# An attention and gated-MLP kernel on one core: another opening order, value tiles all in paired halves, and a last tile in column halves

## The chip, the core and the metric

The kernel runs on one NeuronCore of a Trainium2 chip. The core has TensorE (matrix products, here with its weight loads shown apart), VectorE, ScalarE, GpSimd and SyncE, which issues the DMA transfers; 16 DMA engines move the data. The metric is the device time of one execution in microseconds (us). Beside the timed runs there is one profiled execution, and all views of the profile come from that one.

## The reference, cut to what matters

```python
def reference(A_x, A_wqkv, A_wo, B_x, B_w_gate, B_w_up, B_w_down, gate_w):
    x = A_x                                                 # 2048 x 512
    g = _sigmoid((x * gate_w).sum(-1, keepdims=True))
    a = _A_ref(x, A_wqkv, A_wo)       # attention, 32 heads of 16: softmax(q k / 4) v, then wo
    b = _B_ref(x, B_w_gate, B_w_up, B_w_down)   # (sigmoid(x w_gate) * (x w_up)) w_down, 1792 wide
    return g * a + (1 - g) * b
```

All inputs are fp32.

## The kernel before, in words

Every fp32 operand of a large product is split into a high part in fp32r and a low part, the rest (`split`, line 108). A product of two such operands is the sum of three: high x high, high x low, low x high (`terms`, line 143). A product with 128 contraction rows uses the whole height of the array; one with 64 rows uses half of it, and two such products on different halves can run side by side. `Sum` (line 152) makes a sum of such halves: `half(0)` uses the lower 64 rows, `half(1)` the upper. Two sums are run as a pair, one on its lower rows while the other is on its upper rows; then they change sides. Both halves of a sum write one PSUM bank, so at the change `turn` (line 172) has the next products wait for a token, an empty GpSimd instruction that itself waits for the last product of the first side.

The stages, in order:

1. **Opening (lines 78 to 94, 243 to 257).** TensorE runs products of zeros while the first data arrive (26 in three forms). SyncE loads the first 128 columns of the Q weights, two contraction tiles of the first 512 tokens, the first 128 columns of the K weights, and the other tiles. ScalarE makes the high parts, VectorE the low ones. GpSimd sets the Q and K buffers (`QS`, `KS`: two of each, 128 x 2048) to their start values.
2. **First projections (lines 582 to 602).** For four chunks of 512 tokens, 12 products each for the first Q and K columns (96 in all). `put_first` splits each result and writes it to DRAM (`q_d`, `k_d`); after every second chunk `load_pair` (line 235) reads those tokens back into `QS` and `KS`, head by head, in 12 transfers.
3. **Value tiles with the first maxima (lines 635 to 661).** The value projection makes 16 tiles of 128 tokens, 24 half products each (or 12 whole ones). In between stand the first row maxima: `first_max` (line 575) takes the next step of a list of 40; a step makes two 48-row score products (one for each of two heads, on different halves of the array) into two of the four `sm` banks, and VectorE reduces each to a maximum. The maxima of the first half of the queries are packed by VectorE and GpSimd (`put_max`, line 290) and sent through DRAM into a row of `QS`. Four score products of the first loop step are made ahead in the last pair (`ahead`).
4. **The loop (from line 827).** 256 steps of score products, exponentials on ScalarE, products with the values, later maxima and the remaining projections. A step is 5.6 us.
5. **The end (from line 943).** The down projection in chunks of 512 tokens, `down` holding one bank for each of four token tiles, over 14 tiles of the hidden width; `finish` mixes the result with the attention part and stores it.

TensorE, ScalarE, VectorE and GpSimd run their instructions in the order of the program (line 50); SyncE's transfers are put in order by the planner of the framework.

The loop of stage 3, before:

```python
    for t in range(2):
        o = bankv()
        product(o, tokens(t))
        put_v(t, o, act)
    for t in range(2, NS, 2):
        two = [Sum(bankv(), tokens(t + a)) for a in range(2)]
        for g in (LOW, UP):
            first_max()
            for m in range(3 * KT):
                two[0].half(g)
                two[1].half(1 - g)
                if m in (5, 11):
                    first_max()
```

Of the kernel before, what the change touches and what calls it, by code (L numbers as in the profile page):

```python
# [12 lines left out]
F32 = mybir.dt.float32  # L13
F32R = mybir.dt.float32r
AF = mybir.ActivationFunctionType
ALU = mybir.AluOpType
# [8 lines left out]
S, D, H, DH, F = 2048, 512, 32, 16, 1792  # L25
P = 128
# [11 lines left out]
NPER = NSTEP // 2  # L38
FREE = NPER - LEAD // 2
EARLY = 3  # L40
HF = NF // 2
LOW, UP = 0, 1

# [2 lines left out]
def gated_mix(ctx, tc, x, xT, wqk, wv, wo, w_gate, w_up, w_down, gate_w, out):  # L46
# [32 lines left out]
    dve.memset(warm, 0.0)  # L79
    z = warm.bitcast(F32R)  # L80

    def zeros(o, a, b, r=slice(0, P)):
        rows, m, n = r.stop - r.start, o.shape[0], o.shape[1]
        pe.matmul(o, a[r].to_broadcast([rows, m]), b[r].to_broadcast([rows, n]), start=True, stop=True)
    low, up = slice(0, 64), slice(64, P)
    for _ in range(2):
        for c in range(4):
            zeros(banks[2][32 * c:32 * c + VW, :256], warm, warm, low)
        for _ in range(2):
            zeros(banks[1][:, :256], z, z, up)  # L90
    for _ in range(4):
        zeros(banks[1][:, :256], z, z)
    for _ in range(2):
        zeros(banks[2], z, z)
    mpads = [keep.tile([P, 32], F32, name=f"mpad{i}") for i in range(2)]
    mpad = turns(mpads)
    den = keep.tile([P, 512], F32, name="den")
# [7 lines left out]
    def mid(name, dt=F32):  # L105
        return keep.tile([P, 4, 512], dt, name=name, tag="mid", bufs=3)

    def split(h, l, src, hi, lo):
        if hi is act:
            act.activation(h, src, AF.Copy)  # L110
        else:
            hi.tensor_copy(h, src)
        lo.tensor_tensor(l, src, h.bitcast(F32), ALU.subtract)  # L113

    def raw_weights(src, shape, name):
        raw = keep.tile(shape, F32, name=name + "r", tag="wr", bufs=2)
# [26 lines left out]
    def terms(ab):  # L143
        for (ah, al), (bh, bl) in ab:
            yield from ((ah, bh), (ah, bl), (al, bh))
# [55 lines left out]
    def load_x(c, raw=None, ks=range(KT)):  # L201
        raw = raw or mid(f"x{c}")
        for k in ks:
            sp.dma_start(raw[:, k, :], xT[c, k])
        return raw

    def split_x(c, raw, ks=range(KT)):
        cols = slice(c * 512, (c + 1) * 512)
        for k in ks:
            split(xh[:, k, cols], xl[:, k, cols], raw[:, k, :], act, dve)  # L210

    def unit(w, c):
        cols = slice(c * 512, (c + 1) * 512)
        return [((w[0][:, k, :], w[1][:, k, :]), (xh[:, k, cols], xl[:, k, cols])) for k in range(KT)]

    FORM = {0: (0, 1, 0), 1: (0, 0, 1)}

    def put_first(o, dst, c):

        if c % 2:  # L220
            e = [keep.tile([P, 512], F32R, name=f"qe{i}_{c}", tag="er", bufs=6) for i in range(2)]
        else:
            e = keep.tile([P, 2, 512], F32R, name=f"qe_{c}", tag="ev", bufs=2)
            e = [e[:, i, :] for i in range(2)]
        act.activation(e[0], o, AF.Copy)
        dve.tensor_tensor(e[1], o, e[0].bitcast(F32), ALU.subtract)
        for i in range(2):
            sp.dma_start(dst[i, :P, c * 512:(c + 1) * 512], e[i].bitcast(F32))
# [14 lines left out]
    act.activation(g1[:, :1], warm, AF.Exp)  # L243
    ones = v.rearrange("p t (h c) -> p t h c", c=VW)[:, :, :, DH]
    pool.memset(ones, 1.0)
    raw_q = raw_cols(wqk, 0, "q0")
    xr = {0: load_x(0, ks=(0, 1))}
    raw_k = raw_cols(wqk, KT, "k0")
    load_x(0, xr[0], (2, 3))
    w_q = split_weights(raw_q, act, dve)  # L250
    for b in range(2):
        pool.memset(KS[b].bitcast(F32), -1.0)
        pool.memset(QS[b].bitcast(F32), 0.0)
    split_x(0, xr[0], (0, 1))
    w_k = split_weights(raw_k, act, dve)
    split_x(0, xr.pop(0), (2, 3))
    xr.update((c, load_x(c)) for c in range(1, NC))

    stat = {}
    mrow = {}  # L260
# [320 lines left out]

    for c in range(NC):
        if c + 1 < NC:
            split_x(c + 1, xr.pop(c + 1))
# [7 lines left out]
        two = [(bank(), list(terms(unit(w, c))), dst) for w, dst in ((w_q, q_d), (w_k, k_d))]  # L592
        for part in ((0, 6), (6, 12)) if c == 0 else ((0, 12),):
            for o, ops, dst in two:
                for m in range(*part):
                    pe.matmul(o, *ops[m], start=(m == 0), stop=(m == len(ops) - 1))  # L596
                if part[1] == 12:
                    put_first(o, dst, c)
# [312 lines left out]
    bankh = turns([maxb[0], banks[0], banks[1]])  # L911
    acc, had = {}, {}

    def finish(t, o, gate):

        c = t // 4
        if c not in acc:
            acc[c] = lp.tile([P, 4, D], F32, name=f"acc{c}", tag="acc")
        a = acc[c][:, t % 4, :]
        if (t, 0) in acc:  # L920
            dve.scalar_tensor_tensor(a, o, gate[:, t:t + 1], a, op0=ALU.mult, op1=ALU.add)
# [21 lines left out]
    for n, (c, f) in enumerate(chunks):  # L943
        if f == 0:
            down = [bankt() for _ in range(4)]
        if n in at:
            heads_out(at[n], heads.pop(at[n]))
        hl = ready[n]
        for t in range(4):
            ops = list(terms([((hl[0][:, a, t * P:(t + 1) * P], hl[1][:, a, t * P:(t + 1) * P]), wd[f + a])  # L950
                              for a in range(2)]))
            for m, (a, b) in enumerate(ops):
                pe.matmul(down[t], a, b, start=(f == 0 and m == 0), stop=(f == NF - 2 and m == 5))  # L953
            if (n, t) == (0, 1):
                values(NPER - 1)
                flush(later)
            if f == NF - 2:
                finish(4 * c + t, down[t], g0)
# [49 lines left out]
```

## Time and profile before

| what | value |
|---|---|
| median of 3 runs | 1696.73 us (1695.27 to 1698.48) |
| the profiled execution's own time | 1696.12 us |
| its span | 1694.3 us |
| TensorE, VectorE, ScalarE, GpSimd busy | 1688.6, 1446.0, 1358.7, 881.0 us |
| DMA over the span | 223.51 MB, mean 132 GB/s |

How to read the views: the chain of waits follows the work that ended last back through time, and each of its rows has a start, a length and what ran. A timeline row has start, length, engine, line of the kernel, operation, tile written `<-` tiles read, and how many instructions are taken together; in brackets stands the idle time ahead of it and what ended that. `PE` is a TensorE product, `PEld` its weight load; the ends of products are modelled, so the distance between two starts is what a product costs. A stretch's row has for each engine the busy time and the number of instructions, then the granted TensorE clock, the DMA share and GB/s. Tiles `st`, `dn` and `sm` are PSUM banks, `stat` the maxima, `p` the exponentials, `v` the values.

### The profile page before, as it was taken

What the parts mean: (1) busy time and instruction counts of PE and PEld (TensorE: products, weight loads), DVE (VectorE), ACT (ScalarE), POOL (GpSimd) and SP (SyncE); (2) the same over time, 40 slices, a digit from 0 to 9 for tenths busy, and PEclk for the clock granted to TensorE, in tenths of its full rate; (3) what the DMA queues carried; (4) which work ended last, traced back from release to release, by engine and by line L of the source; (5) the groups of instructions that cost most, each with busy time, mean ns of one, the idle gap of its engine ahead of it and who ended that gap; (6) DMA issues with size and microseconds to landing.
All of it is one profiled execution on the core that took longest, in us unless ns stands there. A gap on an engine that the chain in (4) does not pass through costs nothing.

```text
span 1694.3 us, 34493 instructions
## 1 busy us (share of the span) xinstructions
PE 1688.6 (100%) x12502; PEld 1034.9 (61%) x12502; DVE 1446.0 (85%) x2332; ACT 1358.7 (80%) x2644; POOL 881.0 (52%) x862
## 2 busy tenths in 40 slices
PE   9999999999999999999999999999999999999999
PEld 7755555555555555555555555555555555568887
DVE  6988888888889999999888888889988888888643
ACT  4188888888989888888889889898988989984321
POOL 1034343447665455555566676676666666643110
PEclk9999999999999999999999999999999999999999
DMA  9311424243755342433635353535343434468852
GB/s 256 88 39 58 95 64 96 64 126 134 200 173 145 117 120 89 115 113 103 191 104 139 108 144 102 145 102 130 112 127 108 132 120 128 145 233 280 265 195 72
DMA packets 126666, 223.51 MB, mean 132 GB/s; under 512 B 23264, under 2 KB 33248, under 8 KB 123616
## 3 DMA queue, kind: packets, MB, share of 16 engines
q1 hardware_dynamic: 126496, 221.31, 45.0%
q8 instruction: 98, 1.61, 0.4%
q14 instruction: 72, 0.59, 0.1%
HBM read 131.33 MB, written 89.92 MB: 131 GB/s over the span
## 4 chain that ended last, share of the span: by engine, by line
PE 98%; POOL 1%; DVE 0%; issue 0%; DMA 0%; SPq 0%; POOLq 0%; DVEq 0%
PE dn L163 30%; PE sm L768 27%; PE sm L279 12%; PE st L630 7%; PE sm L953 5%; PE sm L630 5%; PE st L279 2%; PE dn L953 2%; PE st L953 2%; PE st L150 1%; PE st L163 1%; PE st L596 1%; PE sm L150 1%; DVE stat L281 0%; PE st L768 0%
## 5 line engine op out<-in xcount | busy, mean ns | idle before, releaser
L281 DVE TENSOR_REDUCE stat<-sm 128x1 f32<-128x512 f32 x1310 | 848.2, 683 | 152.4 <-PE sm L630 133.2
L632 ACT ACTIVATE p<-st 128x512 f32<-128x512 f32 x1020 | 617.9, 653 | 1.4 <-PE st L630 1.4
L632 ACT ACTIVATE p<-sm 128x512 f32<-128x512 f32 x1026 | 608.8, 630 | 0.6 <-PE sm L630 0.2
L279 PE MATMUL sm<-ks,qs 48*128 48x512 f32 x1310 | 521.7, 437 | 0.2
L281 DVE TENSOR_REDUCE stat<-st 128x1 f32<-128x512 f32 x738 | 482.2, 681 | 0.1
L768 PE MATMUL sm<-p,v 128*17 128x512 f32 x4032 | 482.1, 595 | 0.0
L630 PE MATMUL sm<-qs,ks 64*128 64x512 f32 x1026 | 427.4, 420 | 0.1
L630 PE MATMUL st<-qs,ks 64*128 64x512 f32 x1020 | 426.5, 419 | 0.2 <-DVE stat L281 0.2
L279 PEld LDWEIGHTS sm<-ks,qs 48*128 48x128 f32 x1310 | 238.1, 184 | 293.8 <-DVE stat L281 211.3
L785 POOL TENSOR_TENSOR sum<-sum,part 128x512 f32<-128x512 f32 x224 | 288.9, 1290 | 180.7 <-PE sm L630 173.0
L279 PE MATMUL st<-ks,qs 48*128 48x512 f32 x738 | 291.4, 395 | 0.0
L773 ACT ACTIVATE part<-sm 128x512 f32<-128x512 f32 x215 | 128.7, 599 | 132.4 <-issue 107.4
L768 PEld LDWEIGHTS sm<-p,v 128*17 128x17 f32 x4032 | 93.5, 96 | 227.2 <-issue 157.4
L630 PEld LDWEIGHTS st<-qs,ks 64*128 64x128 f32 x1020 | 187.7, 184 | 30.0 <-issue 3.4
L630 PEld LDWEIGHTS sm<-qs,ks 64*128 64x128 f32 x1026 | 189.1, 185 | 9.8 <-issue 4.3
L507 POOL TENSOR_TENSOR chain<-chain,chain 128x512 f32<-128x512 f32 x84 | 108.5, 1292 | 114.4 <-PE sm L630 108.7
L507 POOL TENSOR_TENSOR had<-chain,had 128x512 f32<-128x512 f32 x84 | 108.1, 1287 | 58.8 <-PE sm L630 46.1
L279 PEld LDWEIGHTS st<-ks,qs 48*128 48x128 f32 x738 | 137.7, 187 | 0.9 <-ACT v L613 0.3
L507 POOL TENSOR_TENSOR side<-side,side 128x512 f32<-128x512 f32 x28 | 36.2, 1291 | 93.3 <-PE sm L630 76.4
L569 ACT ACTIVATE chain<-dn 128x512 f32<-128x512 f32 x112 | 77.9, 696 | 0.0
L113 POOL TENSOR_TENSOR ol<-ot,oh 128x1024 fp32r<-128x1024 f32 (+1 forms) x8 | 16.4, 2054 | 102.5 <-ACT oh L110 82.2
L140 POOL CAST qe<-qk 128x512 fp32r<-128x512 f32 x24 | 14.6, 610 | 77.4 <-ACT qk L569 77.4
(879 smaller groups left out, 3215.0 us busy)
## 6 DMA issues: line engine op xcount, KB each, us to landing
gul<-gu_d SPq DMA_DIRECT2D x56, 512.0 KB
had<-gu_d SPq DMA_DIRECT2D x84, 256.0 KB
gu_d<-had SPq DMA_DIRECT2D x84, 256.0 KB
gu_d<-side SPq DMA_DIRECT2D x56, 256.0 KB
qs<-q_d SPq DMA_DIRECT2D x90, 128.0 KB
ks<-k_d SPq DMA_DIRECT2D x90, 128.0 KB
pv_d<-sum SPq DMA_DIRECT2D x32, 256.0 KB
gu_d<-far SPq DMA_DIRECT2D x28, 256.0 KB
```

Source lines behind the costliest of these rows:

```text
L150: pe.matmul(o, a, b, start=(i == 0), stop=(i == len(ops) - 1))
L163: mm = pe.matmul(self.o, a[rows], b[rows], start=(self.n == 0), stop=(self.n == 2 * len(self.ops) - 1))
L279: pe.matmul(t, qs[r:r + KM, qt * P:(qt + 1) * P], ks[r:r + KM, g * 512:(g + 1) * 512], start=True, stop=True)
L281: dve.tensor_reduce(stat[half][:, b, qt % 8, g:g + 1], t, axis=AX.X, op=ALU.max)
L507: pool.tensor_tensor(to, u, w, ALU.add)
L569: leave = lambda e, o: act.activation(e, o, AF.Copy)
L630: pe.matmul(o, ks[r:r + KR, (kt + a) * P:(kt + a + 1) * P], qs[r:r + KR, q0:q0 + 512], start=True, stop=True)
L632: act.activation(pt[:, 2 * a + c, :], o, AF.Exp, scale=DH ** -0.5)
L768: pe.matmul(o[32 * c:32 * c + VW, :], v[:, 2 * k % 16 + a, h * VW:(h + 1) * VW], pts[c // 2][:, 2 * a + c % 2, :], start=(a == 0), stop=(a ...
L773: act.activation(e, o, AF.Copy)
L785: pool.tensor_tensor(s, s, e, ALU.add)
L953: pe.matmul(down[t], a, b, start=(f == 0 and m == 0), stop=(f == NF - 2 and m == 5))
```

## The change

It edits three places.

- The opening: nine zero products of one form (128 rows, 512 columns) in place of 26. The first weights come in two transfers, each with two of the four contraction tiles of both the Q and the K columns, in place of one transfer for Q and one for K. The first token tile's high part is made by VectorE. The products of the first chunk go contraction tile by contraction tile, Q and K in turn. The four memsets of `QS` and `KS` wait for the last split of the second token chunk.
- The value tiles: all 16 run as eight pairs; the first two, which ran as whole products, are paired as well. A maximum step stands ahead of the half products 0, 5, 10, 15 and 20 of each pair's 24, five steps a pair in place of six. `put_max` follows as soon as its maxima are asked for.
- The end: the last token tile's down projection is made as two halves of 256 columns in two banks, and each half is finished and stored by itself.

```diff
-    def zeros(o, a, b, r=slice(0, P)):
...
-    for _ in range(2):
-        for c in range(4):
-            zeros(banks[2][32 * c:32 * c + VW, :256], warm, warm, low)
-        for _ in range(2):
-            zeros(banks[1][:, :256], z, z, up)
-    for _ in range(4):
-        zeros(banks[1][:, :256], z, z)
-    for _ in range(2):
-        zeros(banks[2], z, z)
+    for _ in range(WARM):
+        pe.matmul(banks[2], z.to_broadcast([P, P]), z.to_broadcast([P, 512]), start=True, stop=True)
...
-    raw_q = raw_cols(wqk, 0, "q0")
-    xr = {0: load_x(0, ks=(0, 1))}
-    raw_k = raw_cols(wqk, KT, "k0")
-    load_x(0, xr[0], (2, 3))
-    w_q = split_weights(raw_q, act, dve)
-    for b in range(2):
-        pool.memset(KS[b].bitcast(F32), -1.0)
-        pool.memset(QS[b].bitcast(F32), 0.0)
-    split_x(0, xr[0], (0, 1))
-    w_k = split_weights(raw_k, act, dve)
-    split_x(0, xr.pop(0), (2, 3))
+    both = wqk.rearrange("(a n) p k f -> n p a k f", a=2)[0]
+    raw, xr, w_qk = [], {}, []
+    for ks in (slice(0, 2), slice(2, 4)):
+        raw.append(raw_weights(both[:, :, ks, :], [P, 2, 2, P], f"qk{ks.start}"))
+        xr[0] = load_x(0, xr.get(0), range(ks.start, ks.stop))
     xr.update((c, load_x(c)) for c in range(1, NC))
+    for i, r in enumerate(raw):
+        w_qk.append(split_weights(r, act, dve))
+        if i == 0:
+            cols = xh[:, 0, :512], xl[:, 0, :512]
+            split(*cols, xr[0][:, 0, :], dve, dve)
+            split_x(0, xr[0], (1,))
+        else:
+            split_x(0, xr[0], (2, 3))
+    w_q, w_k = [[(h[:, i, k, :], l[:, i, k, :]) for h, l in w_qk for k in range(2)] for i in range(2)]
...
         if c == 0:
+            hold = pool.nop()
+            tc.add_manual_dep(hold.ins, last.ins.name, SYNC, reason="memsets behind the first tokens")
+            for b in range(2):
+                pool.memset(KS[b].bitcast(F32), -1.0)
+                pool.memset(QS[b].bitcast(F32), 0.0)
...
+        if c == 0:
+            order = [(i, 3 * k + m) for k in range(KT) for m in (0, 2, 1) for i in range(2)]
+        else:
+            order = [(i, m) for i in range(2) for m in range(3 * KT)]
+        for i, m in order:
+            o, ops, dst = two[i]
+            end = (i, m) == [x for x in order if x[0] == i][-1]
+            pe.matmul(o, *ops[m], start=(m == 0), stop=end)
+            if end:
+                put_first(o, dst, c)
...
-    for t in range(2):
-        o = bankv()
-        product(o, tokens(t))
-        put_v(t, o, act)
-    for t in range(2, NS, 2):
+    for t in range(0, NS, 2):
         two = [Sum(bankv(), tokens(t + a)) for a in range(2)]
         for g in (LOW, UP):
-            first_max()
             for m in range(3 * KT):
+                if (12 * g + m) % 5 == 0:
+                    first_max()
                 two[0].half(g)
                 two[1].half(1 - g)
-                if m in (5, 11):
-                    first_max()
-                if (0, 0) in mrow and g == UP and m == 2:
+                if (0, 0) in mrow:
                     for _, step in put_max((0, 0)):
                         step()
...
-    def finish(t, o, gate):
+    def finish(t, o, gate, s=slice(0, D)):
...
-            dve.scalar_tensor_tensor(a, o, gate[:, t:t + 1], a, op0=ALU.mult, op1=ALU.add)
-            sp.dma_start(out[t * P:(t + 1) * P, :], a)
+            dve.scalar_tensor_tensor(a[:, s], o[:, s], gate[:, t:t + 1], a[:, s], op0=ALU.mult, op1=ALU.add)
+            sp.dma_start(out[t * P:(t + 1) * P, s], a[:, s])
...
             down = [bankt() for _ in range(4)]
+            if c == NC - 1:
+                down.append(maxb[0])
+                bankh = turns([banks[0], banks[1]])
...
-            for m, (a, b) in enumerate(ops):
-                pe.matmul(down[t], a, b, start=(f == 0 and m == 0), stop=(f == NF - 2 and m == 5))
+            both = [(down[t], slice(0, D))]
+            if (c, t) == (NC - 1, 3):
+                both = [(down[3], slice(0, 256)), (down[4], slice(256, D))]
+            for o, s in both:
+                for m, (a, b) in enumerate(ops):
+                    pe.matmul(o[:, s], a, b[:, s], start=(f == 0 and m == 0), stop=(f == NF - 2 and m == 5))
+                if f == NF - 2:
+                    finish(4 * c + t, o, g0, s)
```

More of the change, by code (lines that the diff above doesn't have):

```diff
@@ L40 @@
 EARLY = 3
+WARM = 9
 HF = NF // 2
@@ L80, in gated_mix @@
     z = warm.bitcast(F32R)
-    def zeros(o, a, b, r=slice(0, P)):
-        rows, m, n = r.stop - r.start, o.shape[0], o.shape[1]
-        pe.matmul(o, a[r].to_broadcast([rows, m]), b[r].to_broadcast([rows, n]), start=True, stop=True)
-    low, up = slice(0, 64), slice(64, P)
-    for _ in range(2):
-        for c in range(4):
-            zeros(banks[2][32 * c:32 * c + VW, :256], warm, warm, low)
-        for _ in range(2):
-            zeros(banks[1][:, :256], z, z, up)
-    for _ in range(4):
-        zeros(banks[1][:, :256], z, z)
-    for _ in range(2):
-        zeros(banks[2], z, z)
+    for _ in range(WARM):
+        pe.matmul(banks[2], z.to_broadcast([P, P]), z.to_broadcast([P, 512]), start=True, stop=True)
     mpads = [keep.tile([P, 32], F32, name=f"mpad{i}") for i in range(2)]
@@ L112, in split @@
             hi.tensor_copy(h, src)
-        lo.tensor_tensor(l, src, h.bitcast(F32), ALU.subtract)
+        return lo.tensor_tensor(l, src, h.bitcast(F32), ALU.subtract)
     def raw_weights(src, shape, name):
@@ L209, in split_x, with rows_of @@
         for k in ks:
-            split(xh[:, k, cols], xl[:, k, cols], raw[:, k, :], act, dve)
+            last = split(xh[:, k, cols], xl[:, k, cols], raw[:, k, :], act, dve)
+        return last
+    def rows_of(w, c):
+        cols = slice(c * 512, (c + 1) * 512)
+        return [(w[k], (xh[:, k, cols], xl[:, k, cols])) for k in range(KT)]
     def unit(w, c):
-        cols = slice(c * 512, (c + 1) * 512)
-        return [((w[0][:, k, :], w[1][:, k, :]), (xh[:, k, cols], xl[:, k, cols])) for k in range(KT)]
+        return rows_of([(w[0][:, k, :], w[1][:, k, :]) for k in range(KT)], c)
     FORM = {0: (0, 1, 0), 1: (0, 0, 1)}
@@ L583, in gated_mix @@
         if c + 1 < NC:
-            split_x(c + 1, xr.pop(c + 1))
+            last = split_x(c + 1, xr.pop(c + 1))
         if c == 0:
+            hold = pool.nop()
[3 more added lines that the diff above has]
+                pool.memset(QS[b].bitcast(F32), 0.0)
             wv_r = mid("wv_r")
@@ L591, in gated_mix @@
                 split(wv_h[:, k, :], wv_l[:, k, :], wv_r[:, k, :], act, dve)
[L592 to L598, printed above, removed]
+        two = [(bank(), list(terms(rows_of(w, c))), dst) for w, dst in ((w_q, q_d), (w_k, k_d))]
+        if c == 0:
[8 more added lines that the diff above has]
+                put_first(o, dst, c)
         if c % 2:
@@ L956, in gated_mix @@
                 flush(later)
-            if f == NF - 2:
-                finish(4 * c + t, down[t], g0)
         if n + 4 < len(chunks):
```

## The prediction

> **What bounds the kernel now.** I read the page first, then the chain of waits over the first 130 us, then the timelines of the places that the diff touches.
>
> ```profile
> span 1694.3 us, 34493 instructions
> ...
> PE 98%; POOL 1%; DVE 0%; issue 0%; DMA 0%; SPq 0%; POOLq 0%; DVEq 0%
> ```
>
> TensorE holds 98% of the chain. From about 91 us on nothing in the diff touches the loop until the last tile, so what counts is how far the start of that loop moves, and the last microseconds. The chain of waits shows the opening (start, length, what):
>
> ```profile
> 0.92 5.48 PE st L84 x26
> 6.40 22.75 PE st L596 x96
> 29.15 2.72 PE dn L150 x12
> ...
> 34.59 0.43 PE sm L279 x2
> ...
> 51.43 1.38 PE st L163 x12
> ...
> 77.38 2.33 DMA max_d<-mhl
> 79.72 0.80 SPq L303
> 80.58 1.94 DMA qs<-max_d
> 82.66 0.47 PE dn L630
> ...
> 91.43 1.84 PE sm L768 x16
> ```
>
> In order: zero products, 96 projections, two plain value tiles (24 products, 34.59 - 29.15 = 5.44 us), then pairs of half-row value products with maxima among them. Twelve half products are six slots: 1.38 / 6 = 0.23 us a slot, and a pair of maxima's products, on the two halves of the rows, takes one slot too. In that stage VectorE sets the pace:
>
> ```profile
> 65.68 9.21 DVE L281 TENSOR_REDUCE stat<-sm 128x1 f32<-128x512 f32 x15
> ```
>
> One reduction each 0.61 us (9.21 / 15), 12 for a pair of value tiles: 7.3 us, against 24 + 6 slots of TensorE, 6.9 us.
>
> The transfers decide when maxima may begin. SyncE's timeline and its waits:
>
> ```profile
> 16.21 1.33 SPq L228 DMA_DIRECT2D q_d<-qe  x2
> ...
> 25.45 3.60 SPq L241 DMA_DIRECT2D qs<-q_d  x6
> 29.09 2.76 SPq L241 DMA_DIRECT2D ks<-k_d  x6
> ...
> SPq L241 <- DMA q_d<-qe: 10.3, 4, 5.2
> ```
>
> The first 1024 tokens of Q are written at 16.2 to 17.5 us but the read back starts at 25.45, after a wait for those writes. The stretches say why (the last two numbers are the DMA share and GB/s):
>
> ```profile
> 15.00:20.00 5.00, 5.00 (x24) 4.14 (x23) 3.26 (x6) 2.84 (x7) 0.00 (x0) 1.00 1.02 344
> 20.00:25.00 5.00, 5.00 (x24) 4.14 (x23) 4.91 (x9) 4.14 (x8) 0.00 (x0) 1.00 1.08 261
> 25.00:30.00 5.00, 5.00 (x24) 4.14 (x23) 1.70 (x4) 1.20 (x2) 0.00 (x0) 1.00 0.80 135
> ```
>
> The DMA engines are full until 25 us, 1.02 and 1.08 of their time: it is a backlog of bytes, not a latency. The twelve reads are then issued 0.46 us apart (2.76 / 6), the last at 29.09 + 2.76 - 0.46 = 31.4; the nearest landings are 2.33 and 1.94 us (above), so the last tokens of K are there at 33.3 to 33.7. The first maximum runs at 34.59, straight behind the plain tiles: they cover the loads almost exactly.
>
> **The start of the change.** Nine zero products of one form replace 26 of three. TensorE's first real products:
>
> ```profile
> 6.19 0.63 PE L596 MATMUL st<-xh,q0h 128*128 128x512 f32 x1
> 6.62 0.63 PE L596 MATMUL st<-xl,q0h 128*128 128x512 f32 x1
> ...
> 8.31 0.40 PE L596 MATMUL st<-xh,q0l 128*128 128x512 f32 x1
> 8.55 0.40 PE L596 MATMUL st<-xh,k0h 128*128 128x512 f32 x1
> ```
>
> 0.43 us apart at first, 0.23 from 8.31 on: the array runs at half speed until then. Nine at 0.43 from 0.92 end at 4.8 us, 1.4 sooner. The operands come next:
>
> ```profile
> 4.18 0.69 DVE L113 TENSOR_TENSOR q0l<-q0r,q0h 128x512 fp32r<-128x512 f32 x1 [3.32 <-ACT q0h L110]
> 8.78 3.33 ACT L110 ACTIVATE xh<-x 128x512 fp32r<-128x512 f32 x5 [0.69 <-DMA x<-in_xT_dram]
> 9.45 3.39 DVE L113 TENSOR_TENSOR xl<-x,xh 128x512 fp32r<-128x512 f32 x5 [0.63 <-ACT xh L110]
> ```
>
> The first token tile's copy moves to VectorE behind the weights' subtraction (ends 4.87): 0.3 to 0.7 us more, so real products start at 5.2 to 5.6 instead of 6.19. The last token tile arrives at 8.78 as before and its copy ends at 9.4; products want it at 5.4 + 18 slots = 9.5 at the earliest, so the feed holds. In the first chunk both sums now end together; ScalarE evicts them behind its token copies, which last until 12.1 (8.78 + 3.33) in any case, so their writes stay where they are. With 0 to 1.0 us less at half speed the projections end 0.6 to 2.0 us sooner, at 27.0 to 28.4. The weights come in 1 KB pieces instead of 2 KB, the same bytes: 0 to 0.5 us. GpSimd's four memsets of the Q and K buffers move:
>
> ```profile
> 3.38 1.80 POOL L253 MEMSET qs<- 128x2048 f32 x1
> ```
>
> Four of 1.8, 7.2 us, now behind 12.84 (9.45 + 3.39), end by 20.1. The loads that need them start at 25.45, so they cost nothing; with the DMA backlog gone they would bind from 20.1 on.
>
> None of this makes the token loads earlier: the DMA engines have the same bytes in the same order. So the whole early gain ends in a wait.
>
> **The value tiles.** The plain tiles are gone and the first instruction of the first pair is a maximum. TensorE takes its instructions in order, so all value products queue behind it, and their evictions on ScalarE too. A row of line 279 shows the sequencer's waits for these loads beginning to be met:
>
> ```profile
> L279 PEldq EVENT_SEMAPHORE  x9: 51/51/51, 32.3 to 53.7; - x9
> ```
>
> The first of them ends at 32.3 (the lower rows' tokens); the upper rows follow at 33.3 to 33.7. I take 33.8 for the start of the pairs, 33.3 to 34.5 as ends: TensorE is idle some 6 us.
>
> A pair then is 24 + 5 slots, 29 x 0.23 = 6.67 us. To it comes the turn: between the halves the upper products wait for a token that GpSimd passes on after the last lower one. Before, two maxima calls stood there (m = 11 and the head of the upper half); now the neighbours are at 10 and 15, and nothing stands there. A turn in the main loop shows its length, the first product behind it being slow:
>
> ```profile
> 89.26 0.39 PE L163 MATMUL dn<-xh,q1l 64*128 64x512 f32 x1
> 89.76 0.50 PE L163 MATMUL dn<-xh,q1h 64*128 64x512 f32 x1
> 90.10 0.40 PE L163 MATMUL dn<-xl,q1h 64*128 64x512 f32 x1
> ```
>
> 0.50 + 0.34 where two slots are 0.46: 0.38 us lost. So 7.05 us a pair on TensorE; VectorE's ten reductions are 6.1 and stop being the bound. Eight pairs: 56.4 us. The four score products ahead of the loop share slots, +0.5 (0 to 0.9). In the pair from tile 12 the turn's token queues on GpSimd behind the packing of the first maxima:
>
> ```profile
> 75.00 0.22 DVE L285 TENSOR_REDUCE mpad<-stat 128x16 f32<-128x64 f32 x1
> ...
> 77.10 0.25 POOL L297 TENSOR_TENSOR mhl<-mt,mhl 128x32 fp32r<-128x32 f32 x1
> ```
>
> The first and the last of four steps of 0.21 to 0.25 us. Two reductions and these four take 1.2 + 0.9 = 2.1 us, where seven slots (1.6) and a bare turn's wait stand: +0.4 (0 to 0.7). What goes: the wait for the maxima's transfer ahead of 82.66, since packing now begins 35 slots and two turns (8.8 us) ahead of the score products and with its transfers needs 2.1 + 2.33 + 0.80 + 1.94 = 7.2. I count slots only, so that is in the sum. End: 33.8 + 56.4 + 0.9 = 91.1.
>
> ```profile
> 4.32 1.35 PEld L84 LDWEIGHTS st<-warm 128*128 128x128 f32 x6 [0.22 <-issue]
> 86.90 0.39 PE L163 MATMUL st<-wv_h,xl 64*128 64x512 f32 x1
> ```
>
> Restart at half speed: no row of this trace shows TensorE idle for 6 us. The nearest is the cold start. Zero products on all rows began at 4.32, full pace came at 8.31: 4.0 us at half speed, half of it lost, 2.0 us. Ends: 0 (the array keeps its pace) and 3.7 (cold from 0.92 to 8.31). I take 2.0: the idle stretch is nearly as long as the whole cold start.
>
> The Trainium skill, "TensorE: Matmul & The Clock Gate", Part 1, speaks for this: after about 3.4 us without work the array falls to half its clock, and needs about 3.4 us of work to come back, which by its figure would make the loss 1.7 instead of 2.0 and the sum 0.3 less.
>
> So the loop starts at 93.1; before, the last value product had its slot from 86.90 to 87.13. Shift: +6.0 us.
>
> **The last tile.** Its products come as 84 of 256 columns instead of 42 of 512. The weight row above has six loads of 0.33 in 1.35 us beside 256-column products: they overlap, so 0 (0 to 0.5 us). The bank that it takes leaves two for the heads' sums of the last chunk, which come two steps apart: 0. At the end:
>
> ```profile
> 1683.59 0.19 PEld L953 LDWEIGHTS dn<-wd_l,hl 128*128 128x128 f32 x1
> ...
> 1690.58 0.75 DVE acc L921
> ```
>
> Half of the 0.75 us is left behind the last product, and half as many bytes: -0.5 us (-0.2 to -0.8).
>
> The same page of the Trainium skill, Part 3, speaks against this edit: a weight load overlaps a running product only where the row groups differ. By that rule 42 more loads of 0.19 would stand alone, 8.0 us, and the sum would be 1710. The pitch of 0.23 us with such loads between all products contradicts it here; the third rival goes that way by rows.
>
> **Sum.** 6.0 - 0.5 = +5.5 us on the profiled execution, whose time is 1696.1 (span 1694.3 and 1.8 around it): 1701.6. That execution lies 0.6 under the median of 1696.7, so 1702.2; I say 1702. Own range, from the ends above (clock -2.0 to +1.7, start -0.5 to +0.7, the rest 0.7 either way): 1699 to 1705.
>
> **Rivals.**
>
> *The tokens land sooner (not slower).* SyncE's order is made by a planner, not by hand. If the 1 MB of value weights goes behind the token writes, the read back starts about 3.0 us sooner (1 MB at 344 GB/s), the idle stretch shrinks to about 3 us and the pace holds: 1702 - 3.0 - 2.0 = 1697; with no wait at all 33.8 becomes 27.5 and the time 1702 - 6.3 - 2.0 = 1694. It decides once the reads start before 22.5 instead of 25.45. For it: the planner may see other due times, as memsets moved. Against: the DMA share is full and the program order of these transfers stays. 22%.
>
> *The reads go later.* The same planner sees the memsets end late and puts the writes of the third token chunk ahead of the reads. That is 1 MB at 261 GB/s, 4.0 us more: 1706. For it: their place is free; against: by 20.1 us all is ready. 10%.
>
> *Weight loads bind under 256 columns.* If a 256-column product lasts as long as its weight load: 84 x 0.19 - 42 x 0.23 = +6.3, so 1708. For it: 0.19 (line 953 above) exceeds the 0.115 of half a slot; against: the overlap shown, loads of 0.33 at a pitch of 0.2. 4%.
>
> **Chances.** Forecast 60%, the rivals 22, 10 and 4, others 4. A change under 0.2% (3.4 us) can't be told from none. Faster: the first rival's end without a wait, and a little of the others: 9%. Same: the rest of that rival, and the forecast's part below 1700.1 (clock kept): 32%. Slower: 59%. The range leaves out about 10% at each end: 1695.5 to 1707.
>
> **What would show it.** Right: line 279's first product near 33.8 behind some 6 us without TensorE, products 0.43 us apart behind it, pairs 7.05 us apart, a gap in each at the turn, the first values of the loop near 97 instead of 91.4. Wrong: reads of line 241 that start well before 25 us, VectorE without idle time among the maxima, or pairs nearer 6.7 us; for the end, 256-column products more than 0.12 us apart.

## The result, and the profile after

| kernel | median us (lowest to highest) | runs | ratio, 95% interval |
|---|---|---|---|
| before | 1696.89 (1695.27 to 1698.65) | 6 | |
| after | 1706.01 (1703.55 to 1707.22) | 6 | 1.0051 (1.0038 to 1.0064) |

The change makes the kernel slower by some 9 us. The forecast was 1702.0, slower, in 1695.5 to 1707: the side is right and the time lies in the range, but by the medians the loss is 9.1 us and not 5.3, and 1706.0 lies above the range of 1699 to 1705 that the forecast gave for its own mechanism. The profiled execution took 1706.40 us; its page begins (span; busy time, share and instructions of each engine):

```profile
span 1704.6 us, 34596 instructions
PE 1691.0 (99%) x12551; PEld 1037.3 (61%) x12551; DVE 1448.1 (85%) x2334; ACT 1358.3 (80%) x2643; POOL 881.5 (52%) x862
```

TensorE is still nearly all of the span, so the place to look is again the start of the loop. The chain of waits after (start, length, what):

```profile
17.10 9.92 DMA q_d<-qe
...
30.90 2.90 DMA ks<-k_d
33.91 1.30 PE sm L276 x2
...
87.68 0.33 SPq L107
88.11 0.81 SPq L300
...
91.41 0.46 PE dn L636
...
100.55 1.84 PE sm L769 x16
```

Before, the chain ran almost wholly through TensorE and VectorE from 0.92 us to the packing of the maxima at 75. Now most of its first 34 us are transfers and SyncE's issues of them: TensorE has nothing to do until the tokens of K are back (`ks<-k_d`). The loop's values begin at 100.55 instead of 91.43: 9.12 us of the 10.3 by which the span grew.

TensorE's rows around the wait:

```profile
27.79 0.39 PE L602 MATMUL st<-xh,qk2l 128*128 128x512 f32 x1
...
33.91 1.30 PE L276 MATMUL sm<-ks,qs 48*128 48x512 f32 x2 [5.73 <-DMA ks<-k_d]
...
35.02 0.63 PE L153 MATMUL st<-wv_h,xh 64*128 64x512 f32 x1
...
35.44 0.63 PE L153 MATMUL st<-wv_l,xh 64*128 64x512 f32 x1
```

The last projection starts at 27.79, the first maximum at 33.91: TensorE is idle for 5.73 us of that (the number in brackets), close to the 6 that were forecast. The products of one sum (`st`) then come 0.42 us apart (35.02, 35.44) instead of 0.23. The stretches show how long that lasts (busy time of TensorE, weight loads, VectorE, ScalarE and GpSimd with their instructions; then granted clock, DMA share, GB/s):

```profile
27.00:33.00 6.00, 1.18 (x6) 0.64 (x4) 0.69 (x1) 0.60 (x1) 0.00 (x0) 1.00 0.71 136
33.00:36.00 3.00, 2.09 (x9) 1.66 (x11) 1.28 (x2) 0.00 (x0) 0.00 (x0) 0.52 1.06 274
36.00:39.00 3.00, 3.00 (x18) 2.52 (x16) 1.29 (x3) 0.00 (x0) 0.00 (x0) 0.50 1.12 246
39.00:42.00 3.00, 2.89 (x21) 2.10 (x19) 1.29 (x2) 0.00 (x0) 0.00 (x0) 0.85 1.14 184
```

A mean clock of 0.52, 0.50 and 0.85 in three stretches of 3 us means half speed for 2.88 + 3.00 + 0.90 = 6.8 us, from 33.1 to 39.9 (the trace's record of the clock has the fall at 33.09 and the return at 39.92). VectorE, which set the pace before, is busy for less than half of each stretch.

The other end of the value stage, on GpSimd, SyncE and TensorE:

```profile
83.83 0.34 SPq L296 DMA_DIRECT2D max_d<-mhl  x1
...
85.76 0.35 SPq L107 DMA_DIRECT2D q2r<-in_wqk_dram  x1
...
86.37 1.29 POOL L127 TENSOR_TENSOR k1l<-k1r,k1h 128x512 fp32r<-128x512 f32 x1
...
87.68 0.33 SPq L107 DMA_DIRECT2D k2r<-in_wqk_dram  x1
...
88.11 3.10 SPq L300 DMA_DIRECT2D qs<-max_d  x4
...
91.41 0.46 PE L636 MATMUL dn<-qs,ks 64*128 64x512 f32 x1 [1.07 <-DMA qs<-max_d]
```

The maxima are packed by 83.8 (GpSimd's last step starts at 83.55) and their write is issued at 83.83. Their read back is issued only at 88.11, 4.28 us later. Between the two on SyncE stand two loads of the next weights, `q2r` and `k2r`. They take buffers that GpSimd is still reading: `k1l` ends at 87.66 (86.37 + 1.29), `k2r` is issued at 87.68. So the score product at 91.41 waits, which the prediction had ruled out.

The times of the 40 maxima steps in the trace give the value stage pair by pair. A pair starts with its first maximum (the upper rows' product); the end of the last is taken 4.23 us ahead of the loop's first values product (100.48), as the last value slot stood before (87.13 and 91.36). The chain's rows for these products, 100.55 and 91.43, begin 0.07 later than the products; lengths from a first maximum are counted to the product itself.

| | forecast | after |
|---|---|---|
| first maximum, upper rows | 33.8 | 34.45 |
| first pair | 7.05 + 2.0 | 9.67 |
| each of the next five | 7.05 | 7.08 |
| pair from tile 12 | 7.05 + 0.4 | 7.41 |
| last pair | 7.05 + 0.5 | 9.31 |
| end of the stage | 93.1 | 96.25 |

At the end of the kernel, the chain of waits:

```profile
1700.02 0.71 PE dn L961 x6
1700.73 0.73 PE sm L961 x6
...
1701.49 0.48 DVE acc L922
```

The last tile's 12 products of 256 columns take 0.71 + 0.73 = 1.44 us, where six of 512 columns took 1.37; the last multiplication takes 0.48 instead of 0.75.

### The profile page after: what moved, and what is told of

The parts are those of the page before. It is cut to its first block, busy times and chain, and to the rows that moved or that the text cites. A ratio compares the mean times of both kernels' runs of the same rounds, so it can differ in the third digit from the quotient of the medians.

```text
span 1704.6 us, 34596 instructions
## 1 busy us (share of the span) xinstructions
PE 1691.0 (99%) x12551; PEld 1037.3 (61%) x12551; DVE 1448.1 (85%) x2334; ACT 1358.3 (80%) x2643; POOL 881.5 (52%) x862
## 4 chain that ended last, share of the span: by engine, by line
PE 96%; DMA 1%; DVE 1%; SPq 1%; POOL 0%; ACT 0%; issue 0%; POOLq 0%; DVEq 0%
PE dn L153 29%; PE sm L769 27%; PE sm L276 12%; PE st L636 7%; PE sm L961 5%; PE sm L636 5%; PE st L276 3%; PE dn L961 2%; PE st L153 2%; PE st L961 2%; PE st L140 2%; DMA q_d<-qe 1%; DVE stat L278 1%; PE sm L140 0%; PE st L769 0%; DMA x<-in_xT_dram 0%
## 5 line engine op out<-in xcount | busy, mean ns | idle before, releaser
L504 POOL TENSOR_TENSOR had<-chain,had 128x512 f32<-128x512 f32 x84 | 108.2, 1288 | 56.8 <-PE sm L636 46.0
L504 POOL TENSOR_TENSOR side<-side,side 128x512 f32<-128x512 f32 x28 | 36.2, 1291 | 93.1 <-PE sm L636 82.1
L303 POOL CAST mhl<-mt 128x32 fp32r<-128x32 f32 x32 | 7.5, 234 | 111.8 <-DVE mt L284 111.8
```

What stands on the lines that cost most here:

```text
L504: pool.tensor_tensor(to, u, w, ALU.add)
```

## The experiments

**Which edit carries the loss.** Four kernels put the edits apart. The first is the kernel before with the new value stage alone.

```diff
-    for t in range(2):
-        o = bankv()
-        product(o, tokens(t))
-        put_v(t, o, act)
-    for t in range(2, NS, 2):
+    for t in range(0, NS, 2):
...
-            first_max()
             for m in range(3 * KT):
+                if (12 * g + m) % 5 == 0:
+                    first_max()
```

> The kernel before with the change's value stage alone (eight pairs, five maxima each; opening and end as before). Theory (the token loads bind, TensorE idles and restarts at half clock): the first maximum still runs at 33.9 us, TensorE has nothing to do from 29.2 on, the loop's first values product comes at 99 to 101 us instead of 91.4, and the time is 8 to 10 us over the kernel before. Rival A (the opening is what costs): loop start 91 to 92, time within 1 us. Rival B (the clock keeps its pace over an idle stretch of 4.7 us): loop start near 97.

Measured: 1705.30 us, ratio 1.0045 (1.0032 to 1.0057), by which the loss is 7.6 us; 8 to 10 were expected. The loop's values begin at 99.83, as expected. TensorE's rows at the wait:

```profile
29.15 0.39 PE L596 MATMUL st<-xh,k0l 128*128 128x512 f32 x1
32.52 0.47 PE L279 MATMUL sm<-ks,qs 48*128 48x512 f32 x1 [2.98 <-DMA ks<-k_d]
33.74 0.76 PE L279 MATMUL sm<-ks,qs 48*128 48x512 f32 x1 [0.75 <-DMA ks<-k_d]
```

With the old opening the last projection starts later (29.15 instead of 27.79), and the idle stretch is shorter (2.98 us), but the second product of the pair still starts at 33.74 and at half speed (0.76; the clock falls at 33.11). The value stage alone carries the loss, as far as the intervals tell it from that of the whole change. What the opening gains is idle time.

The reverse: the kernel after with the value stage of before.

```diff
-    for t in range(0, NS, 2):
+    for t in range(2):
+        o = bankv()
+        product(o, tokens(t))
+        put_v(t, o, act)
+    for t in range(2, NS, 2):
...
+            first_max()
             for m in range(3 * KT):
-                if (12 * g + m) % 5 == 0:
-                    first_max()
```

> The changed kernel with the value stage of before (two plain tiles, then seven pairs with six maxima); opening and end stay changed. Theory: the plain tiles run from 27.2 to 32.7, about 1 us idle, no half clock, loop start 90.8 to 91.4, time within 1 us of the kernel before: the opening's two microseconds end in the wait. Rival (opening or column halves cost): loop start right, but the time 2 us or more over before; or loop start over 93.

Measured: 1700.35 us, ratio 1.0011 (1.0003 to 1.0020). Its chain of waits:

```profile
5.90 23.70 PE st L602 x96
29.60 2.72 PE dn L140 x12
32.32 2.72 PE st L140 x12
35.04 0.66 PE sm L276 x2
...
91.94 1.84 PE sm L774 x16
```

The plain tiles fill the wait without a gap and the loop begins at 91.94. Most of the loss is gone; 1.9 us are left, more than was expected of the opening and the halves, and its loop starts only 0.5 us later than that of before. In this profiled execution much of the rest lies late in the loop, where TensorE waits once for a read back of later maxima:

```profile
1472.53 0.47 PE L636 MATMUL sm<-qs,ks 64*128 64x512 f32 x1 [1.84 <-DMA qs<-max_d]
```

The clock is 0.50 for 3.41 us soon after it (1473.74 to 1477.16), and the loop takes 5.0 us longer than before; in the profiles before and after TensorE is nowhere in the loop idle for more than 0.41 us at a time. One profile doesn't show whether the timed runs have such a wait. The two remaining edits were run alone. The opening (zero products, first weights, order of the first chunk, memsets):

```diff
-    for _ in range(2):
-        for c in range(4):
-            zeros(banks[2][32 * c:32 * c + VW, :256], warm, warm, low)
...
+    for _ in range(WARM):
+        pe.matmul(banks[2], z.to_broadcast([P, P]), z.to_broadcast([P, 512]), start=True, stop=True)
...
+    both = wqk.rearrange("(a n) p k f -> n p a k f", a=2)[0]
...
+            hold = pool.nop()
```

> The kernel before with the changed opening alone (zero products, weights by contraction tiles, first token tile on VectorE, memsets later). Theory: the first maximum waits for the same token loads, so the loop starts within 0.5 us of 91.4 and the time stays within 1 us. Rival (the opening costs by itself, as the 1.9 us of the kernel with the value stage put back hint): loop start 92 to 93, time 1.5 to 2 us over before.

Measured: 1700.27 us, ratio 1.0008 (1.0000 to 1.0017); loop's values at 91.66. The start of the loop is that of before within 0.3 us. The interval touches no change, so whether the opening costs 1 us elsewhere stays open; its profile, too, has a wait late in the loop for maxima (1.22 us, ahead of 1470.79).

The column halves:

```diff
+            both = [(down[t], slice(0, D))]
+            if (c, t) == (NC - 1, 3):
+                both = [(down[3], slice(0, 256)), (down[4], slice(256, D))]
+            for o, s in both:
+                for m, (a, b) in enumerate(ops):
+                    pe.matmul(o[:, s], a, b[:, s], start=(f == 0 and m == 0), stop=(f == NF - 2 and m == 5))
```

> The kernel before with the last tile's column halves alone. Theory: each of the seven steps of the last chunk costs 0.1 us more (0.7 in all) and the tail after the last product is 0.6 shorter: time within 0.3 us of before. Rival (weight loads bind): some 6 us more.

Measured: 1697.81 us, ratio 0.9997 (0.9988 to 1.0006). Products and weight loads of its last tile:

```profile
1692.62 0.19 PEld L960 LDWEIGHTS sm<-wd_h,hl 128*128 128x128 f32 x1
1692.74 0.28 PE L960 MATMUL sm<-wd_h,hl 128*128 128x256 f32 x1
1692.86 0.28 PE L960 MATMUL sm<-wd_l,hl 128*128 128x256 f32 x1
```

Products start 0.12 us apart (1692.74, 1692.86) with a load of 0.19 for each: loads overlap products and each other. What lies behind the last product falls from 3.80 to 3.18 us, and the seven steps of the last chunk are each 0.07 to 0.1 longer. The halves give nothing and cost nothing that these runs can show.

**The half clock.** The idle stretch is filled with zero products, so that the wait stays and the array has work.

```diff
     ahead = st_part(0, 1)
+    for _ in range(27):
+        pe.matmul(maxb[3], z.to_broadcast([P, P]), z.to_broadcast([P, 512]), start=True, stop=True)
     for t in range(0, NS, 2):
```

> The changed kernel with 27 products of zeros (512 columns, 6.1 us) ahead of the first maximum, so that TensorE is busy through the wait. Theory (half clock after the idle stretch costs 3.3 us): products 0.23 us apart from the first pair on, loop start at 97.2 instead of 100.5, time 3 us under the changed kernel. Rival (the first pair is slow for another reason, its transfers or its order): loop start stays at 100.5.

Measured: 1705.22 us, ratio 1.0038 (1.0025 to 1.0052). The stretches that ran at half speed in the kernel after, here:

```profile
33.00:36.00 3.00, 2.78 (x15) 1.98 (x15) 0.85 (x2) 0.00 (x0) 0.00 (x0) 1.00 0.89 253
36.00:39.00 3.00, 3.00 (x27) 2.53 (x23) 2.38 (x4) 0.00 (x0) 0.00 (x0) 1.00 1.15 212
```

The clock stays full; the first pair takes 7.17 us instead of 9.67. From its first maximum (35.33) to the loop's values it is 63.3 us instead of 66.0, a gain of 2.7 in place of the 3.3 expected. The first maximum itself came 0.9 later in this profile, as the token reads began at 26.81 and not at 25.54, so the loop's values begin at 98.63, not at the 97.2 expected. The intervals of this kernel and of the kernel after overlap, so the timed runs by themselves don't show the gain.

**The turn.** The maxima are moved so that one of them stands at the change of sides.

```diff
-                if (12 * g + m) % 5 == 0:
+                if (12 * g + m) % 5 == 2:
                     first_max()
```

> The changed kernel with the maxima steps at half products 2, 7, 12, 17 and 22 instead of 0, 5, 10, 15 and 20: the one at 12 stands behind the turn and covers one slot of its wait. Theory (0.4 us of each turn is bare): pairs 6.85 us apart instead of 7.08, loop start 1.5 to 2.2 us sooner, 98.3 to 99. Rival (VectorE or the slots set the pair's length): pairs stay at 7.08.

Measured: 1705.85 us, ratio 1.0044 (1.0032 to 1.0057). Two pairs, first here and then in the kernel after:

```profile
49.88:63.64 13.76, 13.76 (x120) 10.76 (x117) 12.70 (x21) 2.17 (x5) 0.00 (x0) 1.00 0.83 150
```

```profile
51.20:65.36 14.16, 13.93 (x118) 10.78 (x116) 12.70 (x21) 2.18 (x4) 0.00 (x0) 1.00 0.53 121
```

A pair takes 6.88 instead of 7.08 with the same work, and the 0.23 us in which TensorE stood idle in two pairs are gone. The loop's values begin at 98.54, 1.9 sooner; 0.6 of that is an earlier first maximum (33.86). So about half of the turn's 0.41 us (7.08 less 29 slots) can be covered by one slot. The gain is too small for the timed runs to show.

**The maxima's read back.** The work that fetches and splits the next weights is put off by one pair, so that no weight load stands between the maxima's write and their read back.

```diff
-            if t >= 12:
+            if t >= 14:
                 work(1.3)
```

> The changed kernel with GpSimd's splitting of the next Q and K weights held back from the seventh pair to the eighth. Theory (the maxima's read back stands on SyncE behind the load of the next weights, which waits for that splitting): the read back starts right after the maxima's write lands, near 85.5 instead of 88.1, TensorE no longer waits ahead of the first score product, loop start 99.3 to 99.5 instead of 100.5. Rival (the wait is the transfers' own latency): loop start stays at 100.5.

Measured: 1705.91 us, ratio 1.0045 (1.0033 to 1.0058). SyncE and the first score product:

```profile
84.91 0.34 SPq L296 DMA_DIRECT2D max_d<-mhl  x1
86.39 2.92 SPq L300 DMA_DIRECT2D qs<-max_d  x4
91.25 0.39 PE L636 MATMUL dn<-qs,ks 64*128 64x512 f32 x1
```

GpSimd's splitting now begins at 92.04. The read back follows the write by 1.48 us instead of 4.28, and the score product no longer waits. The last pair takes 8.0 us instead of 9.31. The loop's values begin at 100.24 all the same, since the first maximum came 0.85 later in this profile; counted from there it is 64.9 us instead of 66.0. The mechanism is as expected; the absolute start was missed.

**All three together.** Zeros in the wait, the maxima at the turn and the later work, in the kernel after (the three edits above).

> The changed kernel with three of its costs taken out together: 27 zero products in the wait, a maxima step behind each turn, the weights' splitting one pair later. Theory (the costs add up): from the first maximum to the loop's first values product it is 66.0 us in the changed kernel and 56.8 before; 2.5 less for the clock, 1.9 for the turns, 1.3 for the read back, so 60.3 here, time 3 to 4 us over before; what is left is value work that used to stand in the wait. Rival (they overlap): over 62.

Measured: 1701.84 us, ratio 1.0030 (1.0020 to 1.0040). From its chain of waits, the loop's values:

```profile
95.31 1.84 PE sm L771 x16
```

From the first maximum (34.20) to the loop's values it is 61.0 us instead of 66.0; 60.3 were expected. The pair from tile 12 has most of the difference: here, and in the run with the maxima at the turn, it takes 7.87 us instead of 7.41, as TensorE waits 0.90 us at its turn for the token, which GpSimd passes on among its steps of packing. By the ratios the three repairs are worth 3.6 us (0.0021 x 1697), though the two intervals just overlap (1.0038 and 1.0040), and 5.1 are left where 3 to 4 were expected, 3.9 of them at the loop's start (95.31 against 91.43). Those are the plain tiles: eight pairs of 6.88 are 55.0 us, seven of 7.30 (the pitch before) were 51.1. The two tiles used to run under the wait for the tokens and now run behind it.

**Can the tokens come sooner?** The 1 MB of value weights is put behind the first token reads, and its split behind the projections. One profiled execution.

```diff
-            wv_r = mid("wv_r")
-            sp.dma_start(wv_r, wv.rearrange("(k p) f -> p k f", p=P))
...
         if c % 2:
             load_pair(0, slice((c - 1) * 512, (c + 1) * 512))
+        if c == 1:
+            wv_r = mid("wv_r")
+            sp.dma_start(wv_r, wv.rearrange("(k p) f -> p k f", p=P))
```

> The changed kernel with the 1 MB load of the value weights issued behind the first token loads instead of ahead of the token writes, and their split after the last projections. Theory (the token loads wait for a backlog of bytes): the reads of the tokens start about 3 us sooner, near 22.5 us, and the first maximum runs near 31 instead of 33.9; the value products then wait for their weights, to about 36, and the time is no better than the changed kernel's. Rival (the reads wait for something else, a latency or the memsets): they start at 25 us or later as before.

Measured: 1708.00 us. Its timeline and its stretches:

```profile
22.31 3.81 SPq L235 DMA_DIRECT2D qs<-q_d  x6
...
30.91 0.72 PE L276 MATMUL sm<-ks,qs 48*128 48x512 f32 x1 [0.58 <-DMA ks<-k_d]
...
36.56 0.79 PE L153 MATMUL dn<-wv_h,xh 64*128 64x512 f32 x1 [4.93 <-ACT wv_h L100]
```

```profile
27.00:33.00 6.00, 2.38 (x8) 1.07 (x6) 0.69 (x1) 0.60 (x1) 0.00 (x0) 0.83 0.66 174
33.00:36.00 3.00, 0.00 (x0) 0.00 (x0) 0.00 (x0) 0.12 (x1) 0.00 (x0) 0.50 1.02 311
36.00:39.00 3.00, 2.44 (x10) 1.72 (x12) 2.46 (x5) 2.07 (x4) 0.00 (x0) 0.50 1.13 215
39.00:42.00 3.00, 3.00 (x20) 2.31 (x18) 2.51 (x6) 0.00 (x0) 0.00 (x0) 0.63 1.10 259
```

The reads start at 22.31 instead of 25.5 and the second product of the first pair of maxima starts at 30.91 instead of 34.45. So the tokens do wait for bytes, 1 MB being worth 3.2 us, and not for the memsets or a latency. But now the value products wait for their weights until 36.56. Half speed lasts 0.34 x 6 + 3 + 3 + 0.74 x 3 = 10.3 us, and the loop's values begin at 102.11.

**A version that beats both.** In the kernel before, the plain tiles stay, and the six maxima of a pair are spread evenly, with the packing asked for at once and the later work of above: three edits, which were not run apart.

```diff
-            first_max()
             for m in range(3 * KT):
+                if m % 4 == 0:
+                    first_max()
...
-                if m in (5, 11):
-                    first_max()
-                if (0, 0) in mrow and g == UP and m == 2:
+                if (0, 0) in mrow:
...
-            if t >= 12:
+            if t >= 14:
```

> The kernel before with the six maxima of a pair spread evenly (half products 0, 4, 8, 12, 16, 20: one behind the turn), packed as soon as they are asked for, and the weights' splitting held back by one pair. Theory: VectorE stays the bound and is fed without gaps, 40 x 1.22 us from 34.9: its last reduction ends near 84 instead of 85.9, loop start 89.4 to 90.4 instead of 91.4, time 1 to 2 us under before. Rival (nothing to gain: TensorE's slots are as long): loop start 91 to 91.5.

Measured: 1696.46 us, ratio 0.9988 (0.9979 to 0.9997): some 2 us faster than the kernel before (0.5 to 3.6 by the interval). Two pairs in the stretch view:

```profile
49.71:63.91 14.20, 14.20 (x124) 11.15 (x121) 14.20 (x25) 2.17 (x4) 0.00 (x0) 1.00 0.68 158
```

A pair takes 7.10 us where it took 7.30. From the first maximum to the loop's values it is 55.0 instead of 56.8 us. VectorE is busy all the time here and was before (in the stretch from 51.0 to 65.2, 14.18 of 14.20 us), as a reduction of 0.68 us overlaps the next by 0.08. The starts of the reductions in the two traces show where the time went: evenly fed, they come 0.598 us apart; before, one in six came 0.60 to 0.73 us after the one ahead of it, which makes 14.68 us for 24 of them (49.20 to 63.88) instead of 14.35. With eleven zero products of the new form as well:

```diff
-    for _ in range(4):
-        zeros(banks[1][:, :256], z, z)
-    for _ in range(2):
-        zeros(banks[2], z, z)
+    for _ in range(11):
+        pe.matmul(banks[2], z.to_broadcast([P, P]), z.to_broadcast([P, 512]), start=True, stop=True)
```

> The kernel before with evenly spread maxima (as measured: 0.9988 of before) and, from the change, zero products of one form, eleven of them. Theory: the clock is up sooner or as soon, the projections end 0.5 to 1 us sooner, the first maximum comes when its tokens land, 34.2 to 35; loop start 89.3 to 90.4; time 1.5 to 3 us under before, at most 1 us better than without the zeros. Rival (the zeros' form matters for more than the clock): slower than without.

Measured: 1695.67 us, ratio 0.9992 (0.9983 to 1.0001). The loop's values begin at 89.44 instead of 90.41, and both first maximum and full clock come sooner (34.41 instead of 35.40, 5.15 instead of 10.14). The timed runs show no difference between the two, and by themselves don't tell this one from the kernel before; the 1.5 to 3 us that were expected are missed.

## Why the prediction was right, and where its sizes were off

**The main step held.** "None of this makes the token loads earlier ... So the whole early gain ends in a wait": the first maximum ran at 33.91 and 34.45, behind 5.7 us without a product, and with the value stage alone the loss was all there. The term was 33.8, the second product 34.45: 0.65 us of the miss.

**The pair held.** 29 slots and a turn of 0.38 were to make 7.05; the pairs are 7.08 apart. The row from the loop was weaker evidence than it looked: between 89.26 and 89.76 four other products ran (89.27, 89.49, 89.50 and 89.72), so TensorE lost no 0.38 us there; it showed only how long the token holds one sum. A bare turn, in the kernel after, has the same two steps with nothing between them:

```profile
54.45 0.39 PE L153 MATMUL dn<-wv_h,xl 64*128 64x512 f32 x1
54.95 0.49 PE L153 MATMUL dn<-wv_h,xh 64*128 64x512 f32 x1
55.28 0.39 PE L153 MATMUL dn<-wv_l,xh 64*128 64x512 f32 x1
```

The tile-12 pair was to cost 0.4 more and cost 0.33. That the maxima had moved away from the turn was the right reading: with one of them there a pair is 6.88.

**The half clock was seen, and sized too small.** The step "half of it lost, 2.0 us" took the cold start's 4.0 us at half speed as measure. The array stayed at half speed for 6.8 us, of which 0.8 to 1.4 us fell into the idle end, and the first pair lost 9.67 - 7.08 = 2.6: 0.6 of the miss. With work in the gap the loss was gone.

The Trainium skill, "TensorE: Matmul & The Clock Gate", Part 1, gives about 3.4 us of sustained work for the return, counted in a free-running window. Here 6.0 us passed from the first product (33.91) to full speed (39.9), and the clock records of the traces fit such a window. In all of them the changes of the clock lie 3.41 us or a whole multiple of it apart: 33.09 and 39.92 here (two), 30.96 and 41.20 with the value weights late (three), 1473.74 and 1477.16 with the plain tiles back (one).

Cut each trace into these pieces of 3.41 us and take TensorE's busy share of each. At full speed, pieces with 0, 3, 5, 14, 34 and 46% were followed by half speed (as were those in which a kernel ends), and none with 50% or more was. At half speed, pieces with 20 to 82% did not bring the full clock back, and each of the six that were busy throughout did. In the kernel after, the piece from 29.68 to 33.09 was empty, that from 33.09 to 36.51 was 76% busy and the next one full: two pieces at half speed. So the loss hangs on where the pieces fall, and a wait shorter than a piece can bring the fall: with the plain tiles back, 1.84 us were enough, in a piece 46% busy. (The busy shares go by modelled ends of products, and the kernels are all of one family.)

**The step that failed is the wait called gone.** "What goes: the wait for the maxima's transfer ..., since packing now begins 35 slots and two turns (8.8 us) ahead" compared two lengths and left out the queue. The write did go early, and the packing had time; the read back stood on SyncE behind two weight loads that waited for GpSimd. The profile before already had one of them in that place:

```profile
77.38 0.35 SPq L299 DMA_DIRECT2D max_d<-mhl  x1
79.28 0.33 SPq L117 DMA_DIRECT2D k2r<-in_wqk_dram  x1
79.72 2.91 SPq L303 DMA_DIRECT2D qs<-max_d  x4
```

So the 2.33 us that the prediction took as the write's own length (77.38 to 79.72) held a wait for `k2r`; with no load between them the two are 1.48 us apart. The last pair took 9.31 instead of 7.55: 1.3 us are that wait (9.31 - 8.0, from the run that put the work later), and the 0.45 that remain are put down to the four score products, taken at 0.5 and by that nearer 0.9 (8.0 - 7.08). Together this is 1.8 of the 3.1 us by which the start of the loop was missed.

**The sum of the start.** 0.65 + 0.59 + 1.76, and 0.03 for each of the first six pairs, less 0.04 for the tile-12 pair, are 3.1; the loop started 9.12 later instead of 6.0. In the profiled executions the span grew by 10.3 us where 5.5 were forecast: 3.1 more at the start of the loop, 0.9 in the loop and 0.7 at the end.

**The halves.** "-0.5 us" was the tail alone, and that came out as 3.80 - 3.17 = 0.63. The products' side, set at 0 (0 to 0.5), cost 7 steps of 0.07 to 0.1: the loads overlap as was said, but twelve products of 256 columns take a little longer than six of 512. Net nothing.

**The rivals.** Neither earlier nor later reads came about: they began at 25.5 as before. The mechanism of the first rival is real (the run with the value weights behind the reads), but the planner didn't do it, and done by hand it opens the next wait. Weight loads do not bind: 0.12 us from product to product beside loads of 0.19, all on full rows. The rule of the Trainium skill, "TensorE: Matmul & The Clock Gate", Part 3, that a load overlaps a product only on other row groups, is contradicted by these rows if taken by itself; the same part also lets a load into the background weight buffer run ahead, which they don't contradict.

**What stays open.** In the profiled executions the loop itself took 0.9 us longer than before (1412.5 against 1411.5 from its first values to its last group of them), which is within what profiles of these kernels differ by (1411.5 to 1416.5, and 1414.1 without the one whose clock fell in the loop). Whether the opening costs about 1 us in the timed runs was not settled.

## What to carry to other kernels

Work that runs while a transfer is awaited is free, however badly it is packed: before it is packed better, ask what TensorE will do in the wait instead, and add the half clock that follows it, even for a wait of 3 us. When a wait is to vanish because its cause moves forward, follow the whole path on each queue that it uses: here the read back was in time by every length and stood behind loads that waited for a buffer that another engine was reading. The part of the idea that paid leaves the cover where it is and spaces the maxima evenly; it was run together with the earlier packing and the later weight work, so the share of each is not shown.

## What the runs showed that was not expected

- After idle stretches of 5.7, 3.0, 4.3 and 4.1 us the array held half speed for the same 6.8 us, in four kernels of this study (the kernel after, the value stage alone, the maxima at the turn, the later work), for 10.3 us where work was sparse, and for 3.4 us where it was dense at once. At the kernel's start full speed came anywhere from 4.5 to 10.4 us, the same opening varying by as much (5.8, 9.4, 4.5 and 10.4 in four profiles). These are the first records of the clock; the views print 1.00 ahead of them.
- Products of 256 columns ran at 0.12 us beside weight loads of 0.19 us each.
- A load on SyncE that waited for its buffer held the transfer behind it: 4.28 us between write and read back instead of 1.48.
